# Attention and an ELU MLP on one core: the first MLP layer over pairs of batches, and extra matmuls in the first batch

## The chip, the cores and the metric

The kernel runs on one core of a Trainium2 chip. Its engines are TensorE (matmuls, PE in the profile, with its weight loads as PEld), VectorE (DVE), ScalarE (ACT), GpSimd (POOL) and SyncE (SP), beside 16 DMA engines. TensorE writes to PSUM, a small memory[...]; VectorE and ScalarE take results from there. The metric is the device time of one launch, in microseconds.

## The reference

Block-causal attention over 8 batches of 8 heads (576 tokens, head dimension 64), followed by a two-layer MLP with ELU between the layers:

```python
# q, k, v: [8, 8, 576, 64] fp32; w_in: [512, 2048]; w_out: [2048, 512]
scores = scale * np.matmul(q, k.transpose(0, 1, 3, 2))
mask = block_i >= block_j                  # blocks of 64 positions
scores = np.where(mask, scores, -1e9)
attn = softmax(scores)
x = np.matmul(attn, v)  # -> tokens x 512 (heads side by side), 4608 tokens
h = x @ w_in
g = np.where(h > 0.0, h, np.exp(np.minimum(h, 0.0)) - 1.0)
out = g @ w_out         # [4608, 512] fp32
```

## The kernel before

For each batch: loads of q, k, v (fp32) with casts to fp16; transposes of q and k on TensorE (T); scores with keys on the partitions (S), exp on ScalarE; attention times v with a column of ones for the row sums (PV); division by the sums on VectorE and a transpose of the result (X), which gives `xT`: features on partitions, tokens along the columns. Then layer 1 (L1) and layer 2 (L2).

The attention of one head, cut to its matmuls:

```python
# S: keys of chunk c against queries q0:q1, 64 rows of contraction
nc.tensor.matmul(out=sp[0:rows, pcol:pcol + w],
    lhsT=qk[base:base + 64, 1, 128 * c:128 * c + rows],
    rhs=qk[base:base + 64, 0, q0:q1], start=True, stop=True)
# ... widths 512; 64 and 448; 320 and 192; 64, each group then exp'd by ScalarE
# PV: 15 matmuls of 65 columns for a head
nc.tensor.matmul(out=po[0:ntok, t, :], lhsT=attnT[0:rows, p0:p0 + ntok],
    rhs=vE[0:rows, c, h, :], start=(c == 0), stop=(c == t))
```

L1 works on one batch, in two halves of 288 tokens (HTOK), for each of 16 chunks of 128 hidden features (fc). The ELU is max(h, min(exp(h), 1) - 1): exp on ScalarE, the rest on VectorE. PSUM pools have two buffers each: `sc` (T, S and X), `hp` (L1), `l2` (L2), `po` (PV).

```python
def l1_seg(bl, fc, u):
    hp = hp_ps.tile([128, HTOK], FP32, tag="hp", ...)
    for dc in range(NDC):                      # 4 chunks of the 512 features
        yield (120.0, 95.0)
        nc.tensor.matmul(out=hp[:, :], lhsT=w_in_sb[:, dc, fc, :],
            rhs=xT_t[bl][:, dc, HTOK * u : HTOK * (u + 1)], ...)
    e = sm_p.tile([128, HTOK], FP32, tag="e", ...)
    nc.scalar.activation(out=e, in_=hp[:, :], func=AF.Exp, bias=0.0, scale=1.0)
    us = sm_p.tile([128, HTOK], FP16, tag="us", ...)
    nc.vector.tensor_scalar(out=us, in0=e, scalar1=1.0, scalar2=1.0,
        op0=ALU.min, op1=ALU.subtract)
    nc.vector.tensor_tensor(out=g_t[bl][:, fc, HTOK * u : HTOK * (u + 1)],
        in0=hp[:, :], in1=us, op=ALU.max)
    # ... 64 columns at the seam of two batches are also copied into str
```

L2 takes 128 tokens at a time, 16 matmuls of 512 columns (`lhsT=g`, `rhs=w_out`), a copy by ScalarE and a store. A batch has 576 = 4 x 128 + 64 tokens; the last 64 of an even batch and the first 64 of the next make one block out of `str`.

The program interleaves, in iteration `it`, the attention of batch `it`, L1 of batch `it - 1` and L2 of batch `it - 2`:

```python
for it in range(B + 2):
    ba  = it     if it < B else -1
    bl1 = it - 1 if 0 <= it - 1 < B else -1
    bl2 = it - 2 if 0 <= it - 2 < B else -1
    # ... generators of attention and MLP; at each step one matmul of the
    # one that lies further behind, by estimated costs
```

A scheduler of the language then fixes the order of instructions on each engine, and may move them across iterations where data allows it.

Of the kernel before, what the change touches and what calls it, by code (L numbers as in the profile page):

```python
# [8 lines left out]
FP16 = mybir.dt.float16  # L9
FP32 = mybir.dt.float32  # L10
AF = mybir.ActivationFunctionType
ALU = mybir.AluOpType
# [3 lines left out]
def kernel(  # L16
# [9 lines left out]
    nc = tc.nc  # L26

    B, H, S, D = q.shape
    NT, DM = out.shape
# [3 lines left out]
    NFC = DFF // 128  # L33
    NDC = DM // 128
    HTOK = S // 2
# [3 lines left out]
    def cs_cnt(cs):  # L39
        return min(128, S - 128 * cs)  # L40
# [17 lines left out]
    x_p = ctx.enter_context(tc.tile_pool(name="xp", bufs=2))  # L58
    g_p = ctx.enter_context(tc.tile_pool(name="gp", bufs=2))
    str_p = ctx.enter_context(tc.tile_pool(name="strp", bufs=2))  # L60
    sm_p = ctx.enter_context(tc.tile_pool(name="sm", bufs=3))
# [3 lines left out]
    hp_ps = ctx.enter_context(tc.tile_pool(name="hpps", bufs=2, space=bass.MemoryType.PSUM))  # L65
    l2_ps = ctx.enter_context(tc.tile_pool(name="l2ps", bufs=2, space=bass.MemoryType.PSUM))
    po_ps = ctx.enter_context(tc.tile_pool(name="pops", bufs=2, space=bass.MemoryType.PSUM))

    ident = konst.tile([128, 128], FP16, name="ident")
# [6 lines left out]
    q16_t = {}  # L76
    k16_t = {}
    vE_t = {}
    xnat_t = {}
    xT_t = {}  # L80
    g_t = {}
    str_t = {}

# [51 lines left out]
    def ldw_ns(kk, mm):  # L135
        return 100.0 * (kk / 128.0) * (0.35 + 0.65 * (mm / 128.0))
# [4 lines left out]
    def gen_att(bi):  # L141
        vE = vE_t[bi]
        xnat_t[bi] = xnat_p.tile([128, NCS, H, D], FP16, tag="xnat", name=f"xnat_{bi}")
        xT_t[bi] = x_p.tile([128, NDC, S], FP16, tag="xT", name=f"xT_{bi}")
        xn = xnat_t[bi]
        poS = pos_p.tile([128, NCS, H, D + 1], FP32, tag="poS", name=f"poS_{bi}")
        rr = rr_p.tile([128, NCS, H, 1], FP32, tag="rr", name=f"rr_{bi}")
# [78 lines left out]

        def stage_PV(h):
            attnT = attnT_h[h]
            po = po_ps.tile([128, NCS, D + 1], FP32, tag="po", name=f"po_{bi}_{h}")
            for t in range(NCS):  # L230
                ntok = cs_cnt(t)
                for c in range(t + 1):
                    rows = cs_cnt(c)
                    p0 = PB[c] + 128 * t - QS[c]
                    yield ((D + 1) * 0.42, ldw_ns(rows, ntok))
                    nc.tensor.matmul(  # L236
                        out=po[0:ntok, t, :],
                        lhsT=attnT[0:rows, p0 : p0 + ntok],
                        rhs=vE[0:rows, c, h, :],
                        start=(c == 0),  # L240
                        stop=(c == t),
                    )
            nc.vector.tensor_copy(  # L243
                out=poS[0:128, 0 : NCS - 1, h, :], in_=po[0:128, 0 : NCS - 1, :]
            )
            nc.vector.tensor_copy(
                out=poS[0:64, NCS - 1, h, :], in_=po[0:64, NCS - 1, :]
            )
# [35 lines left out]
        for st in stages:  # L284
            yield from st

    def gen_moe(bl1, bl2):
        def l1_seg(bl, fc, u):
            hp = hp_ps.tile([128, HTOK], FP32, tag="hp", name=f"hps_{bl}_{fc}_{u}")
            for dc in range(NDC):  # L290
                yield (120.0, 95.0)
                nc.tensor.matmul(  # L292
                    out=hp[:, :],
                    lhsT=w_in_sb[:, dc, fc, :],
                    rhs=xT_t[bl][:, dc, HTOK * u : HTOK * (u + 1)],
                    start=(dc == 0),
                    stop=(dc == NDC - 1),
                )
            e = sm_p.tile([128, HTOK], FP32, tag="e", name=f"e_{bl}_{fc}_{u}")
            nc.scalar.activation(out=e, in_=hp[:, :], func=AF.Exp, bias=0.0, scale=1.0)  # L300
            us = sm_p.tile([128, HTOK], FP16, tag="us", name=f"us_{bl}_{fc}_{u}")
            nc.vector.tensor_scalar(  # L302
                out=us, in0=e, scalar1=1.0, scalar2=1.0, op0=ALU.min, op1=ALU.subtract
            )
            nc.vector.tensor_tensor(  # L305
                out=g_t[bl][:, fc, HTOK * u : HTOK * (u + 1)],
                in0=hp[:, :],
                in1=us,
                op=ALU.max,
            )  # L310
            if u == 0 and bl % 2 == 1:
                nc.vector.tensor_copy(
                    out=str_t[bl // 2][:, fc, 64:128], in_=g_t[bl][:, fc, 0:64]
                )
            if u == 1 and bl % 2 == 0 and bl + 1 < B:
                nc.vector.tensor_copy(
                    out=str_t[bl // 2][:, fc, 0:64], in_=g_t[bl][:, fc, S - 64 : S]
                )

        def l2_blocks(bl):  # L320
            blks = []
            if bl % 2 == 0:
                for j in range(4):
                    blks.append(("g", 128 * j, 128, bl * S + 128 * j))
                if bl + 1 >= B:
                    blks.append(("g", 512, 64, bl * S + 512))
            else:
                blks.append(("s", 0, 128, bl * S - 64))
                for j in range(4):
                    blks.append(("g", 64 + 128 * j, 128, bl * S + 64 + 128 * j))  # L330
            return blks

        def l2_seg(bl, blk):
            kind, c0, ntok, row0 = blk
            l2p = l2_ps.tile([128, DM], FP32, tag="l2", name=f"l2_{bl}_{row0}")
            src = g_t[bl] if kind == "g" else str_t[bl // 2]
            for fc in range(NFC):
                yield (213.0, 95.0)
                nc.tensor.matmul(  # L339
                    out=l2p[0:ntok, :],  # L340
                    lhsT=src[:, fc, c0 : c0 + ntok],
                    rhs=w_out_sb[:, fc, :],
                    start=(fc == 0),
                    stop=(fc == NFC - 1),
                )
            osb = outsb_p.tile([128, DM], FP32, tag="osb", name=f"osb_{bl}_{row0}")
            nc.scalar.copy(out=osb[0:ntok, :], in_=l2p[0:ntok, :])  # L347
            nc.sync.dma_start(out=out[row0 : row0 + ntok, :], in_=osb[0:ntok, :])

        segs = []  # L350
        if bl1 >= 0:
            g_t[bl1] = g_p.tile([128, NFC, S], FP16, tag="g", name=f"g_{bl1}")
            if bl1 % 2 == 0:
                str_t[bl1 // 2] = str_p.tile(
                    [128, NFC, 128], FP16, tag="str", name=f"str_{bl1 // 2}"
                )
            for fc in range(NFC):
                for u in (0, 1):
                    segs.append(("l1", fc, u))
        blks = l2_blocks(bl2) if bl2 >= 0 else []  # L360
        nblk = len(blks)
        l2i = 0
        mixed = []
        n1 = len(segs)
        for i, sgg in enumerate(segs):
            mixed.append(sgg)
            if l2i < nblk and (
                n1 == 0 or (i % max(1, n1 // nblk) == max(1, n1 // nblk) - 1)
            ):
                mixed.append(("l2", l2i, 0))  # L370
                l2i += 1
        while l2i < nblk:
            mixed.append(("l2", l2i, 0))
            l2i += 1
        for sgg in mixed:
            if sgg[0] == "l1":
                yield from l1_seg(bl1, sgg[1], sgg[2])
            else:
                yield from l2_seg(bl2, blks[sgg[1]])

    def step_loads(load_items):
        if not load_items:
# [11 lines left out]
    for f0 in range(0, NFC, WGRP):  # L394
        nc.gpsimd.dma_start(
            out=w_in_sb[:, :, f0 : f0 + WGRP, :],
            in_=moe_w_in.rearrange("(dc p) (fc j) -> p dc fc j", p=128, j=128)[
                :, :, f0 : f0 + WGRP, :
            ],
        )  # L400
    for f0 in range(0, NFC, NFC // 2):
        nc.gpsimd.dma_start(
            out=w_out_sb[:, f0 : f0 + NFC // 2, :],
            in_=moe_w_out.rearrange("(fc p) m -> p fc m", p=128)[
                :, f0 : f0 + NFC // 2, :
            ],
# [3 lines left out]
    MOE_L1_COST = 16000.0  # L410
# [1 line left out]
    STH = 25.0  # L412
    OH = 25.0

    for it in range(B + 2):
        ba = it if it < B else -1
        bl1 = it - 1 if 0 <= it - 1 < B else -1
        bl2 = it - 2 if 0 <= it - 2 < B else -1

        load_items = list(emit_loads(it + 1)[0]) if 0 <= it + 1 < B else []  # L420
        pend_casts = []

        att = gen_att(ba) if ba >= 0 else None
        moe = gen_moe(bl1, bl2) if (bl1 >= 0 or bl2 >= 0) else None

        att_total = ATT_TOTAL_COST
        nblk2 = 0 if bl2 < 0 else (4 if (bl2 % 2 == 0 and bl2 + 1 < B) else 5)
        moe_total = (MOE_L1_COST if bl1 >= 0 else 0.0) + nblk2 * 16 * 238.0

        n_pe_est = (228 if att is not None else 0) + (  # L430
            (128 if bl1 >= 0 else 0) + (80 if bl2 >= 0 else 0)
        )
        n_items = len(load_items) + 15
        load_every = max(1, n_pe_est // max(1, n_items))

# [90 lines left out]
```

The softmax here doesn't subtract the row's maximum and nothing guards it: scores larger than these inputs give would overflow.

## Time and profile before

| | |
|---|---|
| median time, 4 runs | 501.54 us (500.22 to 509.47) |
| span of the profiled run | 499.7 us |
| busy PE / DVE / ACT / POOL | 91% / 64% / 50% / 8% |
| L1 matmuls, 288 columns | 1024, mean 290 ns |
| L2 matmuls, 512 columns | 576, mean 383 ns (512 with g, 64 with str) |
| exp of L1, 288 columns, ScalarE | 256, mean 410 ns |
| min and subtract of L1, VectorE | 256, mean 305 ns |
| max of L1, VectorE | 256, mean 452 ns |
| data moved by DMA | 42.56 MB, mean 85 GB/s |

In the profile a line such as "L292 PE MATMUL" is the work of line 292 of the kernel. L159 is T, L176 is S, L236 is PV, L270 is X, L292 is L1 and L339 is L2. Busy shares are of the whole span. A matmul's duration includes a tail in which the next one is already running, so the step from one start to the next says what a matmul costs. "xN" is the number of instructions merged into one row. PEclk is the TensorE clock as the profile's throttle records give it.

### The profile page before, as it was taken

What the parts mean: (1) busy time and instruction counts of PE and PEld (TensorE: products, weight loads), DVE (VectorE), ACT (ScalarE), POOL (GpSimd) and SP (SyncE); (2) the same over time, 40 slices, a digit from 0 to 9 for tenths busy, and PEclk for the clock granted to TensorE, in tenths of its full rate; (3) what the DMA queues carried; (4) which work ended last, traced back from release to release, by engine and by line L of the source; (5) the groups of instructions that cost most, each with busy time, mean ns of one, the idle gap of its engine ahead of it and who ended that gap; (6) DMA issues with size and microseconds to landing.
All of it is one profiled execution on the core that took longest, in us unless ns stands there. A gap on an engine that the chain in (4) does not pass through costs nothing.

```text
span 499.7 us, 9463 instructions
## 1 busy us (share of the span) xinstructions
PE 457.2 (91%) x3424; PEld 253.5 (51%) x3424; DVE 318.3 (64%) x1080; ACT 251.9 (50%) x589; POOL 42.0 (8%) x269
## 2 busy tenths in 40 slices
PE   0037989999999999999999999999999999999996
PEld 0014544555555655565555555565556545565542
DVE  0024455779776878687777866687657757677730
ACT  2004533865656466835665367535653464445421
POOL 4001100110100011100000011100010010000000
PEclk9999999999999999999999999999999999999999
DMA  9999574345564444315431642000000000010111
GB/s 179 204 215 180 127 149 105 87 105 125 121 138 95 107 103 113 91 46 126 106 96 43 128 94 65 23 30 15 21 23 22 23 21 23 22 43 22 43 62 65
DMA packets 121935, 42.56 MB, mean 85 GB/s; under 512 B 113184, under 2 KB 117280, under 8 KB 121888
## 3 DMA queue, kind: packets, MB, share of 16 engines
q1 hardware_dynamic: 63552, 24.12, 20.0%
q10 hardware_dynamic: 54144, 13.64, 13.1%
q0 software_dynamic: 4192, 4.19, 4.9%
q8 instruction: 27, 0.44, 0.4%
q14 instruction: 20, 0.16, 0.1%
HBM read 36.70 MB, written 9.44 MB: 92 GB/s over the span
## 4 chain that ended last, share of the span: by engine, by line
PE 85%; DMA 10%; DVE 3%; ACT 1%; issue 0%; ACTq 0%; DVEq 0%
PE hps L292 27%; PE l L339 27%; PE s L176 13%; PE po L236 11%; PE tp L159 4%; DMA st_q_None<-in_q_dram 4%; DMA st_v_None<-in_v_dram 4%; PE xtp L270 3%; DMA st_k_None<-in_k_dram 2%; DVE g L305 1%; DVE xnat L258 1%; DVE us L302 1%; ACT e L300 0%; DVE poS L243 0%; DVE qkT L164 0%
## 5 line engine op out<-in xcount | busy, mean ns | idle before, releaser
L292 PE MATMUL hps<-xT,w_in_sb 128*128 128x288 f16 x1024 | 172.9, 290 | 0.5 <-DVE g L305 0.3
L300 ACT ACTIVATE e<-hps 128x288 f32<-128x288 f32 x256 | 104.6, 410 | 125.0 <-PE hps L292 93.3
L339 PE MATMUL l<-w_out_sb,g 128*128 128x512 f16 x512 | 151.5, 383 | 0.0
L292 PEld LDWEIGHTS <-w_in_sb 128*128 128x128 f16 x1024 | 92.3, 98 | 53.5 <-issue 15.3
L305 DVE TENSOR_TENSOR g<-hps,us 128x288 f16<-128x288 f32 x256 | 113.8, 452 | 3.1
L302 DVE TENSOR_SCALAR us<-e 128x288 f16<-128x288 f32 x256 | 77.2, 305 | 59.6 <-ACT e L300 56.1
L176 PE MATMUL s<-qkT 64*128 64x512 f16 (+5 forms) x384 | 89.7, 299 | 4.3 <-DVE qkT L164 2.2
L236 PE MATMUL po<-vE,attnT 128*128 128x65 f16 (+2 forms) x960 | 86.6, 204 | 0.0
L236 PEld LDWEIGHTS <-attnT 128*128 128x128 f16 (+2 forms) x960 | 59.6, 105 | 37.7 <-issue 16.4
L339 PEld LDWEIGHTS <-g 128*128 128x128 f16 x512 | 46.2, 98 | 32.1 <-issue 6.5
L176 PEld LDWEIGHTS <-qkT 64*128 64x128 f16 (+1 forms) x384 | 29.2, 98 | 55.6 <-issue 46.8
L190 ACT ACTIVATE attnT<-s 128x512 f16<-128x512 f32 x64 | 38.2, 597 | 35.2 <-PE s L176 29.2
L243 DVE COPY poS<-po 128x260 f32<-128x260 f32 x64 | 27.3, 426 | 35.4 <-PE po L236 35.0
L212 ACT ACTIVATE attnT<-s 128x512 f16<-128x512 f32 x64 | 38.3, 599 | 12.5 <-PE s L176 12.3
L201 ACT ACTIVATE attnT<-s 128x512 f16<-128x512 f32 x64 | 38.2, 596 | 9.5 <-PE s L176 9.3
L159 PE MATMUL tp<-ident,q 128*128 128x128 f16 (+1 forms) x160 | 19.7, 231 | 22.9 <-ACT q L116 19.8
L347 ACT COPY osb<-l 128x512 f32<-128x512 f32 x36 | 21.1, 585 | 35.4 <-PE l L339 35.3
L118 DVE CAST k<-st_k_None 128x512 f16<-128x512 f32 (+1 forms) x40 | 16.6, 416 | 32.4 <-DMA st_k_None<-in_k_dram 32.4
L164 DVE COPY qkT<-tp 128x576 f16<-128x576 f16 x64 | 28.6, 452 | 12.0 <-PE tp L159 11.7
L116 ACT CAST q<-st_q_None 128x512 f16<-128x512 f32 (+1 forms) x40 | 23.9, 614 | 19.4 <-DMA st_q_None<-in_q_dram 19.4
L194 POOL MEMSET attnT<- 64x64 f16 x64 | 10.4, 162 | 242.3 <-ACT attnT L190 242.3
L258 DVE TENSOR_TENSOR xnat<-poS,rr 128x512 f16<-128x512 f32 x64 | 29.4, 481 | 0.0
(28 smaller groups left out, 230.2 us busy)
## 6 DMA issues: line engine op xcount, KB each, us to landing
out_dram<-osb SPq DMA_DIRECT2D x36, 256.0 KB, 2.0
st_q_None<-in_q_dram SPq DMA_DIRECT2D x32, 256.0 KB, 3.9
st_k_None<-in_k_dram ACTq DMA_DIRECT2D x32, 256.0 KB, 4.2
st_v_None<-in_v_dram SPq DMA_DIRECT2D x16, 256.0 KB, 3.6
st_v_None<-in_v_dram ACTq DMA_DIRECT2D x16, 256.0 KB, 3.2
w_in_sb<-in_moe_w_in_dram POOLq DMA_DIRECT2D x4, 512.0 KB, 13.4
w_out_sb<-in_moe_w_out_dram POOLq DMA_DIRECT2D x2, 1024.0 KB, 28.0
st_q_None<-in_q_dram SPq DMA_DIRECT2D x8, 128.0 KB, 2.9
```

The costliest lines, as they stand in the source:

```text
L159: nc.tensor.transpose(out=tp[:, 128 * cs : 128 * cs + cnt], in_=src[0:cnt, cs, 2 * hc : 2 * hc + 2, :].rearrange("p h d -> p (h d)"), iden ...
L176: nc.tensor.matmul(out=sp[0:rows, pcol : pcol + w], lhsT=qk[base : base + 64, 1, 128 * c : 128 * c + rows], rhs=qk[base : base + 64, 0, q0 ...
L190: nc.scalar.activation(out=attnT[0:128, 0:512], in_=S0[0:128, 0:512], func=AF.Exp, bias=0.0, scale=SCALE,)
L201: nc.scalar.activation(out=attnT[0:128, 512:1024], in_=S1[0:128, 0:512], func=AF.Exp, bias=0.0, scale=SCALE,)
L212: nc.scalar.activation(out=attnT[0:128, 1024:1536], in_=S2[0:128, 0:512], func=AF.Exp, bias=0.0, scale=SCALE,)
L236: nc.tensor.matmul(out=po[0:ntok, t, :], lhsT=attnT[0:rows, p0 : p0 + ntok], rhs=vE[0:rows, c, h, :], start=(c == 0), stop=(c == t),)
L258: nc.vector.tensor_tensor(out=xn[0:ntok, lo:hi, h0 : h0 + 2, :], in0=poS[0:ntok, lo:hi, h0 : h0 + 2, 0:D], in1=rr[0:ntok, lo:hi, h0 : h0 + ...
L292: nc.tensor.matmul(out=hp[:, :], lhsT=w_in_sb[:, dc, fc, :], rhs=xT_t[bl][:, dc, HTOK * u : HTOK * (u + 1)], start=(dc == 0), stop=(dc == ...
L300: nc.scalar.activation(out=e, in_=hp[:, :], func=AF.Exp, bias=0.0, scale=1.0)
L302: nc.vector.tensor_scalar(out=us, in0=e, scalar1=1.0, scalar2=1.0, op0=ALU.min, op1=ALU.subtract)
L305: nc.vector.tensor_tensor(out=g_t[bl][:, fc, HTOK * u : HTOK * (u + 1)], in0=hp[:, :], in1=us, op=ALU.max,)
L339: nc.tensor.matmul(out=l2p[0:ntok, :], lhsT=src[:, fc, c0 : c0 + ntok], rhs=w_out_sb[:, fc, :], start=(fc == 0), stop=(fc == NFC - 1),)
```

## The change

Two things are changed. First, L1 no longer works on one batch at a time but on pairs of batches: `xT` becomes one tile of 1152 columns for two batches, and L1 takes it in groups of 512, 512 and 128 columns[...], instead of four times 288. The first pair keeps the groups of 288, so that its first half can begin before batch 1 is there. The groups of a pair are spread over two iterations, L1 and L2 start later, and the loop has one iteration more. In the last pair the 128-column groups use the `po` banks. Second, matmuls whose results nobody reads are added: 36 before iteration 1 in the code (`warm`), and 4 for each head of batch 0 ahead of its PV (`keep`), all of 512 columns. They are meant to keep TensorE occupied in the opening.

```diff
-        xT_t[bi] = x_p.tile([128, NDC, S], FP16, tag="xT", name=f"xT_{bi}")
+        if bi % 2 == 0:
+            xpair_t[bi // 2] = x_p.tile([128, NDC, 2 * S], FP16, tag="xT", ...)
+        xT_t[bi] = xpair_t[bi // 2][:, :, S * (bi % 2) : S * (bi % 2) + S]
 ...
         def stage_PV(h):
             attnT = attnT_h[h]
+            if bi in (0,):
+                kp = hp_ps.tile([128, 512], FP32, tag="hp", name=f"keep_{bi}_{h}")
+                for _ in range(4):
+                    yield (213.0, 95.0)
+                    nc.tensor.matmul(out=kp[:, :], lhsT=ident[:, :],
+                        rhs=attnT[:, 1024:1536], start=True, stop=True)
 ...
-    def gen_moe(bl1, bl2):
+    def gen_moe(parts, l2bs):
+        CG = [(0, 512), (512, 1024), (1024, 2 * S)]
+        if parts is not None and parts[0] == 0:
+            CG = [(0, HTOK), (HTOK, S), (S, S + HTOK), (S + HTOK, 2 * S)]
+        def l1_seg(a, fc, cg):
+            c0, c1 = CG[cg]
+            w = c1 - c0
+            if a == B // 2 - 1 and cg == 2:
+                hp = po_ps.tile([128, w], FP32, tag="po", ...)
+            else:
+                hp = hp_ps.tile([128, w], FP32, tag="hp", ...)
             for dc in range(NDC):
-                yield (120.0, 95.0)
+                yield (w / 2.4, 107.0)
-                    rhs=xT_t[bl][:, dc, HTOK * u : HTOK * (u + 1)],
+                    rhs=xp2[:, dc, c0:c1],
 ...
+            # max: one piece for groups 0 and 2, two (64 and 448 columns) for
+            # group 1, which straddles the two batches; str copies as before
 ...
-    for it in range(B + 2):
+    for it in range(B + 3):
+        if it == 1:
+            warm_ps = l2_ps.tile([128, DM], FP32, tag="l2", name="warm_ps")
+            for _ in range(36):
+                nc.tensor.matmul(out=warm_ps[:, :], lhsT=ident[:, :],
+                    rhs=q16_t[0][:, 3, :, :].rearrange("p h d -> p (h d)"),
+                    start=True, stop=True)
-        bl1 = it - 1 if 0 <= it - 1 < B else -1
-        bl2 = it - 2 if 0 <= it - 2 < B else -1
+        parts = None
+        if it == 1:
+            parts = (0, 0)
+        elif it % 2 == 0 and it >= 4 and (it - 2) // 2 < B // 2:
+            parts = ((it - 2) // 2, 0)      # group 0 of a pair
+        elif it % 2 == 1 and it >= 3 and (it - 3) // 2 < B // 2:
+            parts = ((it - 3) // 2, 1)      # groups 1 and 2
+        l2bs = [it - 3] if 1 <= it - 3 < B else []
+        if it == 2:
+            l2bs = [0]
 ...
```

More of the change, by code (lines that the diff above doesn't have):

```diff
@@ L80 @@
     xT_t = {}
+    xpair_t = {}
     g_t = {}
@@ L143, in gen_att @@
         xnat_t[bi] = xnat_p.tile([128, NCS, H, D], FP16, tag="xnat", name=f"xnat_{bi}")
-        xT_t[bi] = x_p.tile([128, NDC, S], FP16, tag="xT", name=f"xT_{bi}")
+        if bi % 2 == 0:
+            xpair_t[bi // 2] = x_p.tile(
+                [128, NDC, 2 * S], FP16, tag="xT", name=f"xTp_{bi // 2}"
+            )
+        xT_t[bi] = xpair_t[bi // 2][:, :, S * (bi % 2) : S * (bi % 2) + S]
         xn = xnat_t[bi]
@@ L228, in stage_PV @@
             attnT = attnT_h[h]
+            if bi in (0,):
+                kp = hp_ps.tile([128, 512], FP32, tag="hp", name=f"keep_{bi}_{h}")
+                for _ in range(4):
+                    yield (213.0, 95.0)
+                    nc.tensor.matmul(
+                        out=kp[:, :], lhsT=ident[:, :], rhs=attnT[:, 1024:1536],
+                        start=True, stop=True,
+                    )
             po = po_ps.tile([128, NCS, D + 1], FP32, tag="po", name=f"po_{bi}_{h}")
@@ L285, in gen_att @@
             yield from st
-    def gen_moe(bl1, bl2):
-        def l1_seg(bl, fc, u):
-            hp = hp_ps.tile([128, HTOK], FP32, tag="hp", name=f"hps_{bl}_{fc}_{u}")
+    def gen_moe(parts, l2bs):
[6 more added lines that the diff above has]
+            if a == B // 2 - 1 and cg == 2:
+                hp = po_ps.tile([128, w], FP32, tag="po", name=f"hps_{a}_{fc}_{cg}")
+            else:
+                hp = hp_ps.tile([128, w], FP32, tag="hp", name=f"hps_{a}_{fc}_{cg}")
+            xp2 = xpair_t[a]
             for dc in range(NDC):
-                yield (120.0, 95.0)
+                yield (w / 2.4, 107.0)
                 nc.tensor.matmul(
@@ L298, in l1_seg @@
                 )
-            e = sm_p.tile([128, HTOK], FP32, tag="e", name=f"e_{bl}_{fc}_{u}")
+            e = sm_p.tile([128, w], FP32, tag="e", name=f"e_{a}_{fc}_{cg}")
             nc.scalar.activation(out=e, in_=hp[:, :], func=AF.Exp, bias=0.0, scale=1.0)
-            us = sm_p.tile([128, HTOK], FP16, tag="us", name=f"us_{bl}_{fc}_{u}")
+            us = sm_p.tile([128, w], FP16, tag="us", name=f"us_{a}_{fc}_{cg}")
             nc.vector.tensor_scalar(
@@ L304, in l1_seg @@
             )
[L305 to L313, printed above, removed]
-                )
[L315 to L318, printed above, removed]
+            if len(CG) == 4:
+                pieces = [(2 * a + cg // 2, HTOK * (cg % 2), HTOK * (cg % 2) + HTOK, 0)]
+            elif cg == 0:
+                pieces = [(2 * a, 0, 512, 0)]
+            elif cg == 1:
+                pieces = [(2 * a, 512, S, 0), (2 * a + 1, 0, 1024 - S, S - 512)]
+            else:
+                pieces = [(2 * a + 1, 1024 - S, S, 0)]
+            for bl, l0, l1_, p0 in pieces:
+                nw = l1_ - l0
+                nc.vector.tensor_tensor(
+                    out=g_t[bl][:, fc, l0:l1_],
+                    in0=hp[:, p0 : p0 + nw],
+                    in1=us[:, p0 : p0 + nw],
+                    op=ALU.max,
+                )
+                if bl % 2 == 1 and l0 == 0:
+                    nc.vector.tensor_copy(
+                        out=str_t[a][:, fc, 64:128], in_=g_t[bl][:, fc, 0:64]
+                    )
+                if bl % 2 == 0 and l1_ == S and bl + 1 < B:
+                    nc.vector.tensor_copy(
+                        out=str_t[a][:, fc, 0:64], in_=g_t[bl][:, fc, S - 64 : S]
+                    )
         def l2_blocks(bl):
@@ L350, in gen_moe @@
         segs = []
[L351 to L355, printed above, removed]
-                )
[L357 to L360, printed above, removed]
+        if parts is not None:
+            pa, which = parts
+            if which == 0:
+                g_t[2 * pa] = g_p.tile(
+                    [128, NFC, S], FP16, tag="g", name=f"g_{2 * pa}"
+                )
+                if len(CG) == 4:
+                    str_t[pa] = str_p.tile(
+                        [128, NFC, 128], FP16, tag="str", name=f"str_{pa}"
+                    )
+                for fc in range(NFC):
+                    segs.append(("l1", fc, 0))
+                    if len(CG) == 4:
+                        segs.append(("l1", fc, 1))
+            else:
+                g_t[2 * pa + 1] = g_p.tile(
+                    [128, NFC, S], FP16, tag="g", name=f"g_{2 * pa + 1}"
+                )
+                if len(CG) == 3:
+                    str_t[pa] = str_p.tile(
+                        [128, NFC, 128], FP16, tag="str", name=f"str_{pa}"
+                    )
+                for fc in range(NFC):
+                    segs.append(("l1", fc, 1 if len(CG) == 3 else 2))
+                    segs.append(("l1", fc, 2 if len(CG) == 3 else 3))
+        blks = []
+        for b2 in l2bs:
+            for blk in l2_blocks(b2):
+                blks.append((b2, blk))
         nblk = len(blks)
@@ L376, in gen_moe @@
             if sgg[0] == "l1":
-                yield from l1_seg(bl1, sgg[1], sgg[2])
+                yield from l1_seg(pa, sgg[1], sgg[2])
             else:
-                yield from l2_seg(bl2, blks[sgg[1]])
+                b2, blk = blks[sgg[1]]
+                yield from l2_seg(b2, blk)
     def step_loads(load_items):
@@ L413 @@
     OH = 25.0
-    for it in range(B + 2):
-        ba = it if it < B else -1
-        bl1 = it - 1 if 0 <= it - 1 < B else -1
-        bl2 = it - 2 if 0 <= it - 2 < B else -1
+    for it in range(B + 3):
+        if it == 1:
+            warm_ps = l2_ps.tile([128, DM], FP32, tag="l2", name="warm_ps")
+            for _ in range(36):
+                nc.tensor.matmul(
+                    out=warm_ps[:, :],
+                    lhsT=ident[:, :],
+                    rhs=q16_t[0][:, 3, :, :].rearrange("p h d -> p (h d)"),
+                    start=True,
+                    stop=True,
+                )
+        ba = it if it < B else -1
+        parts = None
[8 more added lines that the diff above has]
+            l2bs = [0]
         load_items = list(emit_loads(it + 1)[0]) if 0 <= it + 1 < B else []
@@ L423 @@
         att = gen_att(ba) if ba >= 0 else None
-        moe = gen_moe(bl1, bl2) if (bl1 >= 0 or bl2 >= 0) else None
+        moe = gen_moe(parts, l2bs) if (parts is not None or l2bs) else None
         att_total = ATT_TOTAL_COST
[L427 to L432, printed above, removed]
+        nblk2 = sum(4 + (1 if (b % 2 == 1 or b + 1 >= B) else 0) for b in l2bs)
+        l1cost = 0.0
+        nl1 = 0
+        if parts is not None:
+            nl1 = 64 if parts[1] == 0 else 128
+            l1cost = 64 * 238.0 if parts[1] == 0 else 64 * (238.0 + 78.0)
+            if parts[0] == 0:
+                nl1 = 128
+                l1cost = 16000.0
+        moe_total = l1cost + nblk2 * 16 * 238.0
+        n_pe_est = (228 if att is not None else 0) + (nl1 + nblk2 * 16)
         n_items = len(load_items) + 15
```

## The prediction

> **What bounds the kernel now.** I read the page first, its busy table and its chain of waits, then the list of waits, then the timeline of TensorE in two places, early and later.
>
> ```profile
> PE 457.2 (91%) x3424; PEld 253.5 (51%) x3424; DVE 318.3 (64%) x1080; ACT 251.9 (50%) x589; POOL 42.0 (8%) x269
> PEclk9999999999999999999999999999999999999999
> PE 85%; DMA 10%; DVE 3%; ACT 1%; issue 0%; ACTq 0%; DVEq 0%
> ```
>
> TensorE makes up 85% of the chain that ended last, DMA only the opening 10%. The list of what TensorE waited for has 19.8 and 8.2 us for the q and k casts at the start, 3.7 us for VectorE's copies, and nothing else over 2.2 us. So after the load it never starves; time can come only from its own work or its own speed. By the PEclk row the speed is full throughout. The timeline of TensorE says otherwise:
>
> ```profile
> 49.55 1.01 PE L176 MATMUL s<-qkT 64*128 64x512 f16 x3
> 50.49 1.01 PE L236 MATMUL po<-vE,attnT 128*128 128x65 f16 x10
> 51.43 0.61 PE L176 MATMUL s<-qkT 64*128 64x320 f16 x2
> ...
> 84.76 0.59 PE L176 MATMUL s<-qkT 64*128 64x512 f16 x3 [0.17 <-ACT attnT L212]
> 85.28 0.67 PE L292 MATMUL hps<-xT,w_in_sb 128*128 128x288 f16 x4
> 85.78 0.70 PE L236 MATMUL po<-vE,attnT 128*128 128x65 f16 x10
> 86.42 0.66 PE L292 MATMUL hps<-xT,w_in_sb 128*128 128x288 f16 x4
> 86.92 0.38 PE L339 MATMUL l<-w_out_sb,g 128*128 128x512 f16 x1
> 87.23 0.39 PE L176 MATMUL s<-qkT 64*128 64x320 f16 x2
> ```
>
> The first column is the start; the step to the next row is the true cost, since durations include a pipelined tail. The same three score matmuls (512+64+448 columns) take 0.94 us at 49.55 and 0.52 us at 84.76, the ten PV matmuls 0.94 and 0.64. Until about 84 us the array runs at half speed. The table of windows agrees: matmuls per us are 100/18 = 5.6 in 36 to 54 us, 167/30 = 5.6 in 54 to 84, and 142/16 = 8.9 in 84 to 100.
>
> **A ledger of TensorE.** In the last L2 block 26 matmuls of 512 columns lie 0.216 us apart:
>
> ```profile
> 489.65 5.78 PE L339 MATMUL l<-w_out_sb,g 128*128 128x512 f16 x26
> ```
>
> (5.78 less one duration of 0.38) / 25 = 0.216 us, that is 512/2.4 + 2.5 ns. Four matmuls of 288 columns take 0.50 us (86.42 to 86.92), so they cost by columns too. Wherever the stationary tile changes shape (64 rows for scores, 128 for L1 and L2, 64 columns for the last PV rows) there is about 0.1 us more: the single L2 matmul at 86.92 takes 0.31 us instead of 0.216 because scores follow it. So: time = columns/2.4 ns + 2.5 ns per matmul + 98 ns per change of shape. I counted columns, matmuls and changes in the program's instruction order. From 83.7 us on: 769,800 columns = 320.8 us, 3138 x 2.5 = 7.8, 708 changes = 69.4; sum 398.0 us. The trace takes 412.5 us (83.7 to the last matmul's start at 496.2), 3.6% more. From the first score matmul (36.7 us) to 83.7 the same ledger with 3.6% gives 25.4 us, where the trace takes 47.0. Some 21 us are lost there to the slow array, 2.2 of them a wait for a VectorE copy.
>
> **What the Trainium skill says.** "TensorE: Matmul & The Clock Gate", Part 1: the array starts at half clock (1.2 GHz) and goes to 2.4 GHz after about 3.4 us of sustained activity, watched in free-running windows. The trace agrees with the two speeds (0.94 and 0.52 us); but here TensorE was almost never idle from 41 us on and the change came only at 84, so thin work (64-row scores, 65-column PV) apparently doesn't count as sustained. The same part, on back-to-back spacing, has columns/2.4 GHz plus about 2.5 ns when warm; the 0.216 us above is that. "Perfetto Trace Analysis", Identifying the Most-Contended Engine, warns that matmul busy share is no measure of distance from the limit; here a half-speed stretch and a full-speed stretch both read as busy.
>
> **The change, part by part.**
>
> (a) Dummy matmuls. 36 warm-ups and 32 keeps of 512 columns. Though the code puts the warm-ups after batch 0, the instruction order of the changed program has them spread through batch 0's transposes and scores: 18 before the first score matmul, 18 after it, seven of these in one run. The first 18 fall where TensorE waits for loads anyway; at half speed they are 18 x 0.43 = 7.7 us in a stretch from 24 to 39 us that has some 3 us of other work. The first score matmul then comes after VectorE has copied the third head pair's q. In the new order that copy stands behind the casts of v chunks 1 and 2, which wait for DMA:
>
> ```profile
> 38.63 0.43 DVE L122 CAST vE<-st_v_None 128x512 f16<-128x512 f32 x1 [0.33 <-DMA st_v_None<-in_v_dram]
> ```
>
> so 39.05 + 0.37 (copy) gives 39.4, and with the warm-ups in line 39.8 us, 3.1 later than before. From 35.5 us on the sequence is dense in 512-column matmuls, so I take full speed from about 41 us: 0.8 us lost instead of 21.
>
> (b) L1 by pairs: 512+512+128 columns instead of 4 x 288. Columns stay the same. 192 fewer matmuls x 2.5 ns = 0.5 us. The order has 683 shape changes after batch 0's attention against 726: 43 x 98 ns = 4.2 us. So wide matmuls as such bring little.
>
> (c) Ledger of the changed program from its first score matmul: 832,064 columns (25,600 of them in 50 dummies) = 346.7 us, 3252 x 2.5 = 8.1, 766 changes = 75.1; sum 429.9, with 3.6% 445.3.
>
> (d) The other engines. ScalarE's exp on 288 columns is 410 ns and on 512 columns (the attention rows) 597; two of 597 and one near 280 make 1.47 us for a pair's chunk against 1.64. VectorE does the same elements with as many pieces. At 64% and 50% busy neither becomes the bound. The chain that frees an L1 bank gets longer: exp 0.60, min/subtract about 0.42 (the k cast, also 512 columns from fp32 to fp16, takes 418 ns), max about 0.69 (xnat, a two-input operation on 512 columns, takes 687 ns), with 0.1 of hand-over 1.8 us after the matmul's end, about 2.0 after its slot. In the tail the new order leaves one L1 group (0.86) and five L2 matmuls (1.08), 1.94 us, before the bank is needed again. That's short by under 0.1 us in some 15 places; with queueing elsewhere I put 2 us.
>
> Sum: 39.8 + 0.8 + 445.3 + 2 = 487.9 for the last matmul's start; the span ends 3.5 us later as before (499.7 - 496.2), and the measured time is 1.8 over the span (501.5 - 499.7): 493.2. I state 494 because (a) has more ways to lose than to gain.
>
> **Rivals.** 1. The gate doesn't open in batch 0, or closes again. For: 44 us of busy TensorE didn't open it before. Against: no 512-column run on 128 rows was there then. The 50 dummies would cost 50 x 0.43 = 21 us with nothing back: 501.5 + 21 + 3 - 5 = about 520. 2. The wide groups starve TensorE: two L1 banks, a chain of 2 us. For: the margin is 1.94 us. Against: the compiled order fills these gaps with L2 matmuls, and the list of waits before has just 0.3 us of L1 on VectorE. At 0.3 us for the 32 groups of the last pair and some more in mixed iterations this adds 10 us: about 504. 3. The dummies lie entirely in waits of batch 0's attention. For: the chain transpose, copy, scores, exp, PV has latency. Against: with the array fast, batch 0's attention is still 19 us of TensorE without dummies, against about 8 x 2.0 = 16 us of exps, so TensorE wouldn't be idle for long. All 10.8 us hidden: about 483.
>
> **Range and chances.** Most weight lies on the ledger with a few us of waits either way: 489 to 501. Faster by 2% means below 491.5; that needs half of the dummies hidden or a smaller surcharge than 3.6%: 0.27. Slower by 2% needs rival 1: 0.03.
>
> **What would show it.** Right: in the timeline scores of 512+64+448 columns step by about 0.52 us from 41 to 45 us on; windows from 45 us with about 9 matmuls per us outside the dummies; batch 0's attention ends near 72 us, as before, while the next 30 us hold much more L1 work; L1 in 512 columns at 0.216 us each; TensorE's waits on VectorE in L1 under 3 us. Wrong: slow steps beyond 50 us (rival 1), or a row of L1 waits on VectorE's max of over 8 us (rival 2), or a span below 485 (rival 3).

## The result and the profile after

| | before | after |
|---|---|---|
| median time | 500.91 us (16 runs) | 498.22 us (11 runs) |
| ratio after / before, 95% interval | | 0.9938 (0.9918 to 0.9959) |
| span of the profiled run | 499.7 us | 496.4 us |
| TensorE matmuls | 3424 | 3300 |

The time lies in the range that was stated, and within 2% as thought most likely; but the gain is 3 us where the prediction had 7.5 (494 against 501.5). Ratios here and below leave out runs that were more than 1.5% above the fastest of the same kernel.

The same parts of the page, for the changed kernel: busy time, clock row, chain of waits by engine.

```profile
PE 459.4 (93%) x3300; PEld 229.8 (46%) x3300; DVE 303.5 (61%) x1032; ACT 243.5 (49%) x541; POOL 43.1 (9%) x269
PEclk9999999999999999999999999999999999999999
PE 88%; DMA 5%; DVE 2%; SPq 1%; ACT 1%; issue 0%; ACTq 0%
```

TensorE is still the bound, more so than before (88% of the chain against 85). The clock row again reads full everywhere, and again the timeline corrects it: the clock records of this run begin with the clock's opening at 45.1 us, and the time before the first record is drawn as full. TensorE in the opening of the changed kernel (first column: start):

```profile
40.01 0.61 PE L181 MATMUL s<-qkT 64*128 64x512 f16 x1
...
41.62 3.17 PE L472 MATMUL warm_ps<-q,ident 128*128 128x512 f16 x7
44.73 0.56 PE L181 MATMUL s<-qkT 64*128 64x320 f16 x2
45.22 0.60 PE L472 MATMUL warm_ps<-q,ident 128*128 128x512 f16 x2
...
46.44 0.60 PE L181 MATMUL s<-qkT 64*128 64x512 f16 x3
46.97 1.04 PE L238 MATMUL keep<-attnT,ident 128*128 128x512 f16 x4
47.85 0.85 PE L249 MATMUL po<-vE,attnT 128*128 128x65 f16 x15
```

Seven warm-ups take 3.11 us to the next row, 0.44 us each: half speed. The four keeps at 46.97 take 0.88, 0.22 each, and the three score matmuls at 46.44 take 0.53: full speed. The array changed at about 45 us instead of 84. The first score matmul starts at 40.0 us (39.8 was predicted). The table of windows of the changed kernel follows. Behind the length of a window stand busy us, with the number of instructions in brackets, of TensorE, its weight loads, VectorE, ScalarE and GpSimd, then the clock, the DMA share and GB/s:

```profile
54.00:84.00 30.00, 28.12 (x238) 14.86 (x238) 20.21 (x66) 15.85 (x36) 3.58 (x26) 1.00 0.64 136
84.00:100.00 16.00, 15.83 (x147) 9.24 (x144) 12.01 (x44) 12.16 (x30) 2.29 (x17) 1.00 0.46 102
```

In 54 to 84 us there are 238 matmuls instead of 167, but 27 of them are dummies. Wide L1 runs as the ledger of the prediction (columns, matmuls and changes of shape, each at its cost) has it:

```profile
395.85 1.25 PE L315 MATMUL hps<-xTp,w_in_sb 128*128 128x512 f16 x8
397.03 0.53 PE L181 MATMUL s<-qkT 64*128 64x320 f16 x3
```

Eight matmuls, 4 x 512 and 4 x 128 columns, take 1.18 us with one change of shape: 2560/2.4 + 8 x 2.5 + 98 ns = 1.185.

What is new stands between 150 and 200 us. Two windows of the kernel before, then the same two of the changed one:

```profile
150.00:175.00 25.00, 25.00 (x208) 14.67 (x208) 18.52 (x66) 13.62 (x33) 1.43 (x11) 1.00 0.45 100
175.00:200.00 25.00, 25.00 (x198) 13.66 (x198) 20.03 (x69) 16.66 (x41) 3.46 (x20) 1.00 0.45 109
```

```profile
150.00:175.00 25.00, 23.08 (x208) 13.19 (x207) 20.37 (x68) 15.88 (x37) 2.84 (x21) 1.00 0.62 127
175.00:200.00 25.00, 24.28 (x213) 13.98 (x213) 19.25 (x69) 15.18 (x38) 2.37 (x18) 1.00 0.39 85
```

TensorE (first busy column) was occupied for all 50 us before, and for 47.36 now. The ledger falls short of the trace in this stretch by 1.1 us before and 5.5 after; below, this difference is called the loss. From start to start, twelve steps of the changed kernel are over 0.08 us longer than the ledger, 4.1 us together, and none is before. The largest, 1.1 us at 157 us, is a wait for VectorE's division (xnat). The list of what TensorE waited for in this stretch has 1.5 us for that division and less than the 4.1 in all, since it counts from a matmul's modelled end and leaves out the pipelined tail. The same windows for the L2 tile alone show what is missing:

```profile
150.00:175.00 25.00, 8.72 (x31) 1.00 0.45 100
175.00:200.00 25.00, 8.21 (x26) 1.00 0.45 109
```

```profile
150.00:175.00 25.00, 3.82 (x10) 1.00 0.62 127
175.00:200.00 25.00, 4.37 (x14) 1.00 0.39 85
```

57 L2 matmuls before (first table), 24 after. VectorE is about as busy in both kernels (38.55 and 39.63 us). L2 works on results of an earlier iteration, so it can fill TensorE's waits; the experiments below test that. The change gives iteration 3 no L2 of its own (`l2bs` starts again in iteration 4) and half of pair 0's L1. That pair has groups of 288 columns, so no wide group stands in this stretch.

### The profile page after: what moved, and what is told of

Read it like the earlier page. It is cut to its first block, busy times and chain, and to the rows that moved or that the text cites. A ratio compares the mean times of both kernels' runs of the same rounds, so it can differ in the third digit from the quotient of the medians.

```text
span 496.4 us, 9057 instructions
## 1 busy us (share of the span) xinstructions
PE 459.4 (93%) x3300; PEld 229.8 (46%) x3300; DVE 303.5 (61%) x1032; ACT 243.5 (49%) x541; POOL 43.1 (9%) x269
## 4 chain that ended last, share of the span: by engine, by line
PE 88%; DMA 5%; DVE 2%; SPq 1%; ACT 1%; issue 0%; ACTq 0%
PE hps L315 27%; PE l L372 27%; PE s L181 13%; PE po L249 11%; PE tp L164 5%; DMA st_v_None<-in_v_dram 5%; PE xtp L283 3%; PE warm_ps L472 2%; PE keep L238 2%; SPq L107 1%; DMA st_k_None<-in_k_dram 1%; DVE xnat L271 1%; ACT attnT L217 0%; DVE poS L256 0%; DVE qkT L169 0%
## 5 line engine op out<-in xcount | busy, mean ns | idle before, releaser
L315 PE MATMUL hps<-xTp,w_in_sb 128*128 128x512 f16 (+2 forms) x832 | 157.1, 315 | 1.0 <-DVE g L338 0.9
L323 ACT ACTIVATE e<-hps 128x512 f32<-128x512 f32 (+1 forms) x208 | 92.0, 463 | 108.8 <-PE hps L315 98.2
L372 PE MATMUL l<-w_out_sb,g 128*128 128x512 f16 x512 | 141.4, 381 | 0.0
L338 DVE TENSOR_TENSOR g<-hps,us 128x288 f16<-128x288 f32 (+4 forms) x256 | 111.1, 450 | 1.7
L325 DVE TENSOR_SCALAR us<-e 128x512 f16<-128x512 f32 (+1 forms) x208 | 67.0, 339 | 63.9 <-ACT e L323 63.3
L315 PEld LDWEIGHTS <-w_in_sb 128*128 128x128 f16 x832 | 69.8, 98 | 64.4 <-issue 12.3
L181 PE MATMUL s<-qkT 64*128 64x512 f16 (+5 forms) x384 | 82.6, 283 | 1.3 <-DVE qkT L169 0.3
L249 PE MATMUL po<-vE,attnT 128*128 128x65 f16 (+2 forms) x960 | 78.5, 199 | 0.0
L249 PEld LDWEIGHTS <-attnT 128*128 128x128 f16 (+2 forms) x960 | 55.2, 101 | 32.5 <-issue 13.7
L372 PEld LDWEIGHTS <-g 128*128 128x128 f16 x512 | 44.8, 97 | 39.2 <-issue 4.5
L181 PEld LDWEIGHTS <-qkT 64*128 64x128 f16 (+1 forms) x384 | 27.6, 96 | 56.3 <-issue 48.1
L164 PE MATMUL tp<-ident,q 128*128 128x128 f16 (+1 forms) x160 | 18.7, 223 | 19.9 <-ACT q L117 19.7
L199 POOL MEMSET attnT<- 64x64 f16 x64 | 10.2, 159 | 219.6 <-ACT attnT L195 219.6
## 6 DMA issues: line engine op xcount, KB each, us to landing
w_out_sb<-in_moe_w_out_dram POOLq DMA_DIRECT2D x2, 1024.0 KB, 27.8
```

What stands on the lines that cost most here:

```text
L164: nc.tensor.transpose(out=tp[:, 128 * cs : 128 * cs + cnt], in_=src[0:cnt, cs, 2 * hc : 2 * hc + 2, :].rearrange("p h d -> p (h d)"), iden ...
L181: nc.tensor.matmul(out=sp[0:rows, pcol : pcol + w], lhsT=qk[base : base + 64, 1, 128 * c : 128 * c + rows], rhs=qk[base : base + 64, 0, q0 ...
L315: nc.tensor.matmul(out=hp[:, :], lhsT=w_in_sb[:, dc, fc, :], rhs=xp2[:, dc, c0:c1], start=(dc == 0), stop=(dc == NDC - 1),)
L338: nc.vector.tensor_tensor(out=g_t[bl][:, fc, l0:l1_], in0=hp[:, p0 : p0 + nw], in1=us[:, p0 : p0 + nw], op=ALU.max,)
L372: nc.tensor.matmul(out=l2p[0:ntok, :], lhsT=src[:, fc, c0 : c0 + ntok], rhs=w_out_sb[:, fc, :], start=(fc == 0), stop=(fc == NFC - 1),)
```

## The experiments

Theory A: the early clock is the gain, the dummies cost nearly as much, L1 by pairs saves its changes of shape and gives them back in iteration 3. Rival B: L1 by pairs is the gain and the dummies come to nothing.

### The dummies alone

```diff
 # the kernel before, L1 by halves of one batch, plus:
+  stage_PV, batch 0:  4 keeps of 512 columns for each head
+  before iteration 1: 36 warm-ups
```

> The kernel before plus the 36 warm-ups and 32 keeps, L1 unchanged. Theory A (the gain is the early clock less the cost of the dummies, and L1 by pairs adds about nothing): array at full speed from about 45 us, ledger of TensorE from the first score matmul 435.2 us, so 498 to 499.5 us. Rival B (the gain is L1 by pairs, the dummies cost what they bring): about 501.

Measured: 498.91 us, ratio 0.9941 (0.9919 to 0.9963). The array is at full speed from 41.0 us by the trace's clock records, and the timeline agrees, with 1.62 us for the seven warm-ups instead of 3.11:

```profile
41.74 1.68 PE L427 MATMUL warm_ps<-q,ident 128*128 128x512 f16 x7
43.36 0.39 PE L176 MATMUL s<-qkT 64*128 64x320 f16 x2
```

The parts add up against the trace of the kernel before: by 85 us the loss, counted from the first score matmul, is 4.0 instead of 22.9 us (18.9 won); the ledger is 12.7 us longer (435.2 against 422.5); the first score matmul comes at 40.6 instead of 36.7 us (3.9 lost). 18.9 - 12.7 - 3.9 = 2.3 us, and the last matmul starts at 492.78 instead of 495.05. So the dummies aren't hidden: most of what the clock brings is spent on opening it. Set beside this kernel, the change has a ledger 5.3 us shorter (429.9), but its last matmul starts only 1.0 us earlier (491.75): it loses 4.2 us more between 150 and 200 us, and its clock opened later, which costs 2.1 us.

### The pairs alone

```diff
 # the changed kernel without the dummies
-  36 warm-ups before iteration 1
-  4 keeps for each head of batch 0
```

> The changed kernel without any dummy matmuls. Theory A: slow array until about 80 us as before; the ledger is 3.2 us shorter than before, but 4 to 5 us of new waits between 150 and 200 us eat that: 500 to 502 us. Rival B: about 498.

Measured: 499.95 us, ratio 0.9974 (0.9958 to 0.9990). Full speed only from 88.5 us. The stretch from 150 to 200 us loses 4.2 us, without a dummy in the kernel, so the loss belongs to the rearranged MLP. A is right on the first kernel and within 0.1 us of its range on this one, B is right on neither: the larger part of the gain is the clock's, though pairs bring a little, about 1.3 us.

### Warm-ups without keeps

```diff
-            if bi in (0,):
-                kp = hp_ps.tile([128, 512], ...)
-                for _ in range(4): ...            # no keeps
```

> The changed kernel with the 36 warm-ups but without the 32 keeps. If the clock, once open at about 45 us, stays open without them, the ledger loses 6 us: 492 us. If the keeps are what holds it open, scores of 512+64+448 columns step by 0.94 us again within batch 0 and the time is 500 or more.

Measured: 502.74 us, ratio 1.0005 (0.9987 to 1.0024). The profiled run is one of its longer ones (509.8 us); its clock row:

```profile
PEclk9999655569999999999999999999999999999999
```

The clock opened at 41.1 us, closed at 54.7, and came back at 109.3 (the row's slices are 12.7 us). In its timeline the three score matmuls take 0.52 us at 51.96 and 0.95 at 58.30:

```profile
51.96 0.59 PE L181 MATMUL s<-qkT 64*128 64x512 f16 x3
52.48 0.71 PE L241 MATMUL po<-vE,attnT 128*128 128x65 f16 x10
...
58.30 1.01 PE L181 MATMUL s<-qkT 64*128 64x512 f16 x3
59.25 1.01 PE L241 MATMUL po<-vE,attnT 128*128 128x65 f16 x10
```

In the other 22 runs the mean clock is 0.957 to 0.973, so it closed in them too. The 32 keeps are therefore no ornament: here the warm-ups open the clock, and without the keeps it doesn't stay open.

### Keeps without warm-ups

```diff
-            for _ in range(36): ...               # no warm_ps
```

> The changed kernel with the 32 keeps but without the 36 warm-ups. If four 512-column matmuls a head are dense enough to open the clock, it opens at 45 to 55 us and the time is 494 to 497 us; if not, it opens near 80 us and the keeps cost twice their length: 506 us or more.

Measured: 497.37 us, ratio 0.9883 (0.9846 to 0.9921); single times lie at 493.7 and 493.8 and at 497.3 to 497.7, one at 509. In the profiled run the clock opens at 56.1 us, a little later than the 45 to 55 us expected, and the time is 0.4 us above its range. The ledger is 4.5 us shorter, the first score matmul 2.3 us earlier (37.7 us), the loss to the slow array larger. That the times fall in groups fits a clock that opens at one step or another (below).

### The MLP spread otherwise

```diff
-        if it == 1:
-            parts = (0, 0)
+        if it in (1, 2):
+            parts = (0, it - 1)          # pair 0's second half in iteration 2
 ...
-        l2bs = [it - 3] if 1 <= it - 3 < B else []
+        l2bs = [it - 3] if 2 <= it - 3 < B else []
 ...
+        # L2 of batch 1: blocks 0 to 2 in iteration 3, 3 and 4 in iteration 4
```

> The changed kernel with the MLP work of the first iterations spread otherwise: the second half of pair 0's L1 in iteration 2 instead of 3, L2 of batch 1 cut in three blocks in iteration 3 and two in iteration 4. If the 5.5 us that TensorE lost between 150 and 200 us come from an iteration with 32 L1 groups and little L2 to fill their waits, the loss there falls to about 1.5 us; the ledger is 1.8 us longer, so 495.5 us. If the waits belong to L1 by pairs as such, 498 to 500.

Measured: 497.50 us, ratio 0.9929 (0.9899 to 0.9959). The loss between 150 and 200 us falls to 1.5 us as expected; its windows and, after them, those of its L2 tile:

```profile
150.00:175.00 25.00, 25.00 (x199) 14.37 (x197) 19.94 (x70) 13.78 (x33) 1.20 (x9) 1.00 0.56 120
175.00:200.00 25.00, 24.77 (x193) 12.22 (x190) 14.02 (x43) 16.82 (x38) 4.02 (x23) 1.00 0.44 108
```

```profile
150.00:175.00 25.00, 9.28 (x32) 1.00 0.56 120
175.00:200.00 25.00, 8.69 (x30) 1.00 0.44 108
```

VectorE is as busy in the first window as in the change (19.94 and 20.37 us), yet TensorE doesn't idle, and 0.5 us are lost instead of 3.2: 32 L2 matmuls stand there instead of 10. In the second window VectorE has less to do than in the change as well (14.02 and 19.25 us), so there the 30 L2 matmuls aren't the only difference. The gain comes back out, though: from 250 to 350 us this kernel loses 6.0 us where the change loses 2.2. At 296 to 312 us it has just 10 L2 matmuls left, and TensorE waits four times for VectorE's max (of six such waits and 3.2 us in the list for the whole run). The L2 work was spent early and lacked later. The time missed the 495.5 us that were expected.

### Dummies before the scores

```diff
 # in stage_T, batch 0, head pair 0, after chunk 3
+        early = {(0, 3): 11, (1, 3): 7}      # behind the 4th q and the 4th k chunk
+        for _ in range(early): nc.tensor.matmul(out=pre[:, :], ...)   # 512 columns
-            for _ in range(36):
+            for _ in range(8):
```

The first of these kernels is called e6_early in the expectations, the second e7_early_keep2; e5_balanced is the kernel of the section before.

> The changed kernel with the dummies moved: 11 directly after the fourth q chunk is transposed and 7 after the fourth k chunk, in waits for loads, and 8 instead of 36 warm-ups; all 26 stand before the first score matmul. Keeps as they are. If dense work before the scores opens the clock there, it opens by 31 us, the ledger from the first score matmul is 425.5 instead of 429.9 us, and the time is 489 to 492. If the waits for loads close it again before the scores, 497 or more.

> As e6_early, with two keeps a head instead of four. If half the keeps still hold the clock open, 2.5 us less than e6_early: 487 to 490. If it closes in batch 0's attention, as it did without keeps, 498 or more.

> e7_early_keep2 with the spread of e5_balanced. If both gains add up: 484 to 487 us. If the clock closes: 496 or more.

Measured: 510.53 us, with times from 497.6 to 513.3; the ratio, 0.9964 (0.9936 to 0.9992), rests on 7 of 22 runs, and the median says more here. With two keeps 503.75 us, 1.0053 (1.0031 to 1.0075); with the other spread as well 501.31 us, 1.0000 (0.9985 to 1.0015). All three missed. In the profiled runs the clock did open at 29.2, 27.8 and 30.7 us, as hoped, but closed at 36.0, 34.6 and 34.1 us, in waits for a k chunk and for VectorE's copies (at 35.19 us after 2.59 us idle in the second). The windows of the second say the rest:

```profile
28.00:35.00 7.00, 2.30 (x12) 0.94 (x11) 1.50 (x4) 0.00 (x0) 0.00 (x0) 0.97 1.22 206
35.00:45.00 10.00, 8.01 (x35) 3.32 (x34) 4.38 (x12) 1.12 (x2) 0.32 (x2) 0.50 1.33 225
45.00:60.00 15.00, 15.00 (x92) 7.17 (x91) 5.61 (x18) 6.20 (x15) 2.15 (x15) 0.50 0.68 119
60.00:92.00 32.00, 32.00 (x183) 15.42 (x183) 15.73 (x50) 13.66 (x29) 2.82 (x20) 0.50 0.44 96
```

With two keeps a head TensorE is busy for every one of the 47 us from 45 to 92 and the clock stays at half. In e6_early, with four, it opened again at 42.9, closed at 46.3, and was open from 59.9 on. So full occupation by itself doesn't open it, and the number of 512-column matmuls a head matters. That it is the work in the array that counts fits this, but isn't shown apart from other differences such as the changes of shape.

### The groups of 288 columns in the new order

```diff
-        if parts is not None and parts[0] == 0:
+        if True:                     # four groups of 288 columns for every pair
             CG = [(0, HTOK), (HTOK, S), (S, S + HTOK), (S + HTOK, 2 * S)]
```

> The changed kernel with all pairs in four groups of 288 columns, as the first pair has; order of work by iteration and dummies as in the change. The ledger of TensorE from the first score matmul is 433.1 instead of 429.9 us (more changes of shape). If width saves just that, 500.5 to 502 us. If wide groups lose it again by longer chains on VectorE and ScalarE, 498 as the change.

Measured: 501.03 us, ratio 0.9995 (0.9977 to 1.0014), 2.8 us over the change where the ledger has 3.2. So width saves about what its fewer changes of shape save; the two profiled runs can't say it more finely, since the clock opened at 40.7 us in this one. In 150 to 200 us it loses 5.4 us, as the change does. That is no test of width, for TensorE's order is the same in both kernels up to 203 us and holds groups of 288 alone; it shows that the loss comes again in another run.

### L2 of batch 0 split between iterations 2 and 3

```diff
-        if it == 2:
+        if it in (2, 3):
             l2bs = [0]
+        l2cut = {2: (0, 2), 3: (2, 4)}.get(it, (0, 5))
 ...
-            for blk in l2_blocks(b2):
+            for blk in l2_blocks(b2)[l2cut[0] : l2cut[1]]:
 ...
```

> The changed kernel with L2 of batch 0 split: two blocks in iteration 2, two in iteration 3, whose 32 L1 groups have no L2 of their own in the change. If the 5.5 us lost between 150 and 200 us are L1 waits without other work to fill them, the loss there falls to 2 us or less; ledger 0.9 us longer; 495 us. Otherwise 499.

Measured: 495.71 us, ratio 0.9893 (0.9865 to 0.9921), times from 495.3 to 497.8. It beats both kernels. The reason is only in part the one expected. The loss between 150 and 200 us falls from 5.5 to 4.05 us, not to 2. Its L2 tile in the two windows:

```profile
150.00:175.00 25.00, 7.40 (x26) 1.00 0.60 133
175.00:200.00 25.00, 3.79 (x12) 1.00 0.45 101
```

With 26 L2 matmuls the first window loses 1.4 us (the change: 10 and 3.2), with 12 the second loses 2.7 (the change: 14 and 2.2), 1.4 us of it in one wait for VectorE's max at 190 us. The loss fell in the window that got the L2 work and not in the other; VectorE had a little less to do in the first, too (18.00 us against 20.37). The rest of the gain between the two profiled runs is not the split's: the clock is open from 39.0 us on, in the change's run from 45.1, and that accounts for some 2.3 us of the 2.7 between the two spans. Up to 120 us the order of instructions on TensorE is the same in both kernels, and in those of the sections on the other spread and on 288 columns, where the clock opened at 39.6 and 40.7 us. So the opening differs from run to run, and the change's profiled run had a late one.

### The split with fewer warm-ups

```diff
 # with the split:
-            for _ in range(36):      # none, and then 18
```

Here e4_no_warm is the kernel with keeps alone, e10_l2_split the one of the section before.

> e4_no_warm with the split of e10_l2_split. If the two are independent: 3 us under e4_no_warm, 493 to 495. If the split brings nothing: 498.

> e10_l2_split with 18 warm-ups instead of 36: these 18 all stand before the first score matmul, none after. If the clock opens at the first scores even so (39 to 41 us), the 18 warm-ups after the scores were pure cost: ledger 426.3 us and 491 to 493 us. If they are needed to open it, it opens at 50 us or later: 496 or more.

Inconclusive as times. Without warm-ups they scatter from 493.3 to 506.5 us (median 502.71; ratio 0.9872, 0.9821 to 0.9924, from 2 of 6 runs), with 18 from 493.1 to 509.0 (median 506.61; ratio 0.9904, 0.9877 to 0.9931, from 6 of 22). In the first's profiled run, one of 506.0 us, the clock opens only at 80.9 us: keeps alone open it early in some runs and not in others. The second's profiled run has 497.1 us and shows what the 18 later warm-ups are for:

```profile
36.00:42.00 6.00, 5.03 (x24) 2.25 (x24) 2.80 (x7) 1.76 (x4) 0.61 (x5) 1.00 1.34 232
43.00:56.00 13.00, 13.00 (x73) 5.90 (x71) 4.00 (x13) 4.14 (x9) 1.26 (x10) 0.50 0.80 132
57.00:70.00 13.00, 12.61 (x106) 6.19 (x104) 7.07 (x24) 10.10 (x23) 2.51 (x16) 1.00 0.75 153
```

The clock opens at 39.2 us, closes at 42.7, and opens again at 56.3. So the warm-ups after the first scores aren't pure cost: in this run the clock didn't last without them. The set of 68 dummies is dear but steadier: times of 496.4 to 500.6 us for the change and 495.3 to 497.8 for the split.

## Why the prediction missed more than half of its gain

The mechanism held: TensorE at half speed until 84 us, dummies that end this at about 45 us, a gain of much less than the 21 us lost there because 50 dummies stand in the way, width worth its changes of shape. The sum was 491.4 us of span; the trace has 496.4. By its terms:

- **First score matmul**, 39.8 us predicted, 40.0 measured: 0.2 us.
- **"Full speed from about 41 us"** in (a): 45.1 in the profiled run, so 2.3 us lost to the slow array instead of 0.8: 1.5 us. Four other kernels with the same opening show 39.0 to 41.0 (dummies alone, the other spread, groups of 288, the split). The estimate was good, and this run unlucky.
- **"With queueing elsewhere I put 2 us"** in (d), and 3.6% on the ledger, together 17.4 us; the trace has 19.7 from 45 us on: 2.3 us. This is the step that failed. I looked for new waits in the tail, at the two PSUM buffers of L1, but TensorE waits there for VectorE's max just 0.9 us in the whole run. I didn't ask what work TensorE would have left, iteration by iteration, when the other engines are late. Around iteration 3, between 150 and 200 us, it had 24 L2 matmuls where it had 57, and 5.5 us were lost instead of 1.1. Two kernels bear out that the filler (the L2 work left for such waits) counts: with 62 L2 matmuls in the stretch 1.5 us are lost, and with 38 the loss falls just in the window that got more. The number of L2 matmuls alone is no rule: from 200 to 225 us, where wide L1 begins, the change has 16 of them and loses 0.5 us. "VectorE does the same elements", so it is no bound, was right as an average and beside the point.
- **The tail**: I took 496.2 us for the start of the last matmul before; the trace has 495.05. So 4.7 us follow it, not 3.5: 1.2 us. The same misreading made the surcharge 3.6% where the trace gives 3.35%, 1.0 us too much, so that it nearly cancels in the sum; read rightly, the third term falls short by 3.3 us instead of 2.3.

Together 5.2 us, against 5.0 between the spans. What (b) said, that wide matmuls as such bring little, is borne out by the 2.8 us that groups of 288 cost. Of the rivals, the second came nearest, but the place was wrong; the first isn't in the profiled run of the change (four other runs, with a mean clock of 0.989 to 0.995, may have had a little of it), but it is in the kernels with fewer dummies; the third is refuted by the sum of the dummies alone. The sign to look for, L1 waits on VectorE under 3 us, was met while most of the loss sat in waits for the division, a copy and exps of attention: too narrow a test. Batch 0's attention ended at 75.2 us, not 72, in good part by the late clock: the split, with the same order and a clock open from 39.0 us, has 73.3.

## What to carry to other kernels

Before you count on interleaving, count per stage how much independent work is left for the bound engine when the others are late: moving L2 away from L1 changed no total and still cost 4 us around one iteration. Read an engine's speed from start to start of equal instructions, early and late; a busy row and a clock row that both read full hid 20 us. If dummy work is to open a clock, count its own time from the start: in the kernel with dummies alone 19 us were won and 17 spent.

## What was unexpected of the hardware

In the clock records of these runs the clock opens and closes in steps of about 3.4 us: before closing again it stayed open 3.4 us (four times), 6.8 us (twice), 10.2 and 13.7 us, and it stayed closed for as long as 58.0 us, 17 steps of 3.41. The Trainium skill, "TensorE: Matmul & The Clock Gate", Why this matters for your kernels, asks for no idle gaps over some 3 us on TensorE to keep the clock; here it stayed at half for 32 us in which TensorE was busy for 32.00 (60 to 92 us, two keeps a head), and closed at 54.7 us in a stretch of scores and PV whose longest listed wait is 0.32 us. So the absence of gaps didn't suffice. Both stretches hold many 64-row scores and 65-column PV with a change of shape between them. Four 512-column matmuls of 128 rows a head held the clock in the change and opened it again at 59.9 us in e6_early; two did neither: in the kernel with two keeps and the other spread the clock closed at 51.1 us and stayed closed to 92.1. Which of the thin rows, the few columns and the changes of shape keeps it closed isn't shown.

The moment of opening isn't fixed by the program: in four profiled runs with the same order of instructions up to 120 us it came between 39.0 and 45.1 us.
